# Local attention scores as 32 queries x 64 keys in two column halves, two small vector steps on GpSimd, and a load ahead of two stores

## The chip, the cores and the metric

The kernel runs on one core of a Trainium2 chip. TensorE (PE) multiplies matrices, VectorE (DVE), ScalarE (ACT) and GpSimd (POOL) work on vectors, SyncE (SP) issues most DMAs. The metric is the device time of one execution in microseconds (us), the median of several.

## What is computed

The inputs are q, k, v of shape (4, 8, 576, 64) (batch, heads, sequence, head width), eight experts' weights and the weights of a last layer.

```python
scores = scale * np.matmul(q, k.transpose(0, 1, 3, 2))          # scale = 1 / 8
rel = pos[:, None] - pos[None, :]
mask_local = (rel >= 0) & (rel < 32)                             # heads 0 to 3
mask_strided = (rel >= 0) & (pos[None, :] % 32 == pos[:, None] % 32)   # heads 4 to 7
scores = np.where(mask, scores, -1e9)
scores = scores - np.max(scores, axis=-1, keepdims=True)
attn = np.exp(scores)
attn = attn / (np.sum(attn, axis=-1, keepdims=True) + 1e-09)
x = np.matmul(attn, v)                                           # 2304 tokens x 512
# each token goes to one of 8 experts: argmax of cosine similarities / tau, weighted by its probability
out[mask] = gate_w[mask, None] * (np.maximum(x[mask] @ w1[e], 0) @ w2[e])
h = np.maximum(np.maximum(x @ w1, x @ w2), x @ w3)               # last layer
return h @ w_out
```

A local query sees only the 32 keys up to its own position.

## The kernel before

The program has three stages: attention with the routing of its tokens (to about 122 us), the experts (to about 346 us) and the last layer. Each engine works through its own list in the order in which the program is written; an instruction that waits holds up all that stand behind it on its engine. Engines wait for each other by semaphores.

**Attention** works through 44 groups, 11 for each of the 4 batches: 5 local ones (four blocks of 64 queries of a pair of heads, the fifth with two blocks) and 6 strided ones (heads are handled separately, in groups of 4, 4 and 2 blocks). `attention` is one loop over steps s, and each step writes a stage of a different group on each engine: scores of group s (`g_scores`: PE), maximum and exponentials of group s-1 (`g_max`, `g_exp`), normalisation of s-2 (`g_norm`), transposes of s-4 (`g_trans`), weighted sum of values of s-5 (`g_av`). Between them come `tok_half` (a matmul that turns the result back into token rows, whose copy to SBUF is written a step later) and the routing of the batch before (`route_stages`).

One step, engine by engine:

- PE: the scores s (L383, for a local group after a matmul that writes the mask, L375), the transposes t (L422), the token rows r (L476), the weighted sum x (L441).
- DVE: maximum mx (L390), its scaled negative nb (L394), sum of the exponentials plus 1e-9, r2 (L411, shown as `r`), reciprocal ri (L413), copy of token rows (L486), copy pt of the transposes (L424), then routing, if there is any.
- ACT: the copy xt of the weighted sum (L451), four exponentials with their row sums rs (L402), squares for the routing (L512).
- POOL: the exponentials times ri (L414), and once a batch the square root of the norms (L528) and an addition (L529).

A local group takes a block's 64 queries of two heads as 128 rows (the query tile `ql` holds zeros in the other head's half of the contraction) and 96 keys, 32 before the block and 64 in it. The keys and queries of a batch have one buffer each, so the loads of the next batch (`load_kq`, on SP's queue) wait for the last scores that read the old ones.

**The experts** and **the last layer** are chains of matmuls in which PE hardly stops. Weights are loaded, split into two parts on ACT and DVE (`w_stages`), and the nine slices of the last layer's first matmul (`UP`) are also stored to `u_scr`, from which they come back for later blocks.

Of the kernel before, what the change touches and what calls it, by code (L numbers as in the profile page):

```python
# [9 lines left out]
F32 = mybir.dt.float32  # L10
# [5 lines left out]
ALU = mybir.AluOpType  # L16
# [3 lines left out]
B, H, S, D = 4, 8, 576, 64  # L20
NT, DM, E, F, F2 = 2304, 512, 8, 1024, 768
NTILE = NT // 128
SCALE = 0.125
# [26 lines left out]
LA = 5  # L50
# [19 lines left out]
def kernel(ctx, tc, a, out, x_scr, w_scr, u_scr, perm_scr, gate_scr, upto="all"):  # L70
    nc = tc.nc
# [34 lines left out]
    UP = range(8 * E, 8 * E + 9)  # L106
# [41 lines left out]
    def w_stages():  # L148

        n = next_split[0]  # L150
        next_split[0] += 1
        t = staged.pop(n)[0]
        u, parts, ws = unit(n), [t], []
        if n in UP:

            (a11, a21), (a12, a22) = ([t.rearrange("p (k c g n) -> p k g c n", k=2, c=2, g=2)[:, k, g] for g in range(2)] for k in range(2))
            sb = pools["sb"].tile([128, 3, 256], F32, tag="sb", name="sb")  # L160
            s1, s2, s4 = (sb[:, i].rearrange("p (c n) -> p c n", c=2) for i in range(3))
            parts.append(sb.rearrange("p i n -> p (i n)"))

        def sums():
            if n in UP:
                for o, x, y, op in ((s1, a21, a22, ALU.add), (a21, a11, a21, ALU.subtract), (s2, s1, a11, ALU.subtract), (s4, a12, s2, ALU.subtract)):
                    nc.vector.tensor_tensor(out=o, in0=x, in1=y, op=op)

        def upper():
            for i, x in enumerate(parts):  # L170
                m = 1024 - 256 * i
                ws.append(slot_tile(u + i))
                nc.scalar.activation(out=ws[i][:, 0, 0:m], in_=x, func=ACTF.Copy)  # L173

        def rest():
            for i, x in enumerate(parts):
                m = 1024 - 256 * i
                nc.vector.tensor_tensor(out=ws[i][:, 1, 0:m], in0=x, in1=ws[i][:, 0, 0:m].bitcast(F32), op=ALU.subtract)  # L178
                if n in UP:
                    nc.sync.dma_start(out=u_scr[n - 8 * E, i, :, :, 0:m], in_=ws[i][:, :, 0:m].bitcast(F32))  # L180
            wsl[n] = ws if n in UP else ws[0]
            ready.add(n)
            w_load()

        return [sums, upper, rest]

# [156 lines left out]
    groups = []  # L343
# [25 lines left out]
    def g_scores(g):  # L369
        b, kind, j, hh = groups[g]  # L370
        ns, nq, nk = shape(g)
        ps = ps_s.tile([128, 512], F32, tag="s", name="s")
        if kind == 0:
            o = 96 if j == 0 else 0 if j == 2 else 192
            nc.tensor.matmul(  # L375
                out=ps[:, 0:ns * nk], lhsT=identb, rhs=mask_l[:, o:o + ns * nk], start=True, stop=False, skip_group_check=True)
        for i in range(ns):
            c, blk = slot(g, i)
            if kind == 0:
                q, k = ql[:, c, 128 * blk:128 * blk + 128], kl[:, c, 64 * blk:64 * blk + 96]  # L380
            else:
                q, k = (t[:, hh, c, 126 * blk:126 * blk + nq] for t in (qs, ks))
            nc.tensor.matmul(  # L383
                out=ps[:nq, i * nk:(i + 1) * nk], lhsT=q, rhs=k, start=kind == 1, stop=kind == 1 or i == ns - 1, skip_group_check=True)
        st[g] = dict(ps=ps)

    def g_max(g):
        ns, nq, nk = shape(g)
        mx = st_p.tile([128, 4], F32, tag="mx", name="mx")
        nc.vector.tensor_reduce(  # L390
            out=mx[:nq, 0:ns], in_=st[g]["ps"][:nq, 0:ns * nk].rearrange("p (s k) -> p s k", s=ns),
            axis=AX.X, op=ALU.max, negate=True)
        nb = st_p.tile([128, 4], F32, tag="nb", name="nb")
        nc.vector.tensor_scalar(out=nb[:nq, 0:ns], in0=mx[:nq, 0:ns], scalar1=SCALE, scalar2=None, op0=ALU.mult)  # L394
        st[g]["nb"] = nb

    def g_exp(g):
# [9 lines left out]
    def g_norm(g):  # L407
        ns, nq, nk = shape(g)
        d = st[g]
        r2 = st_p.tile([128, 4], F32, tag="r2", name="r2")  # L410
        nc.vector.tensor_scalar(out=r2[:nq, 0:ns], in0=d["rs"][:nq, 0:ns], scalar1=1e-9, scalar2=None, op0=ALU.add)  # L411
        ri = st_p.tile([128, 4, 1], F32, tag="ri", name="ri")
        nc.vector.reciprocal(out=ri[:nq, 0:ns, 0], in_=r2[:nq, 0:ns])  # L413
        nc.gpsimd.tensor_tensor(  # L414
            out=d["p"][:nq, 0:ns, :nk], in0=d["p"][:nq, 0:ns, :nk],
            in1=ri[:nq, 0:ns].to_broadcast([nq, ns, nk]), op=ALU.mult)
# [11 lines left out]
    def g_av(g):  # L428
        b, kind, j, hh = groups[g]
        if kind == 1 and hh == 0:  # L430
            return
        ns, nq, nk = shape(g)
        if j == 0:
            xT[b, kind] = xt_p.tile([128, 2, S], F32, tag=f"xt{kind}", name="xt")
        xp = ps_x.tile([128, 512], F32, tag="x", name="x")
        n = nq if kind else 64
        for i in range(ns):
            c, blk = slot(g, i)
            for h2 in range(2):
                pt = st[g - 1 + h2]["pt"][:nk, i, :nq] if kind else st[g]["pt"][:nk, i, 64 * h2:64 * h2 + 64]  # L440
                nc.tensor.matmul(  # L441
                    out=xp[64 * h2:64 * h2 + 64, i * n:(i + 1) * n],
                    lhsT=vv[b, kind][:nk, 2 * c + h2, blk, :], rhs=pt, start=True, stop=True)
        if kind == 0:
            dst = xT[b, 0].rearrange("p c n -> p (c n)")[:, 256 * j:256 * j + 64 * ns]
            src = xp[:, 0:64 * ns]
        else:
            r0, nr = (14 * j, 14) if j < 2 else (28, 4)
            dst = xT[b, 1].rearrange("p c (a r) -> p c r a", r=32)[:, :, r0:r0 + nr, :]
            src = xp[:, 0:ns * nq].rearrange("p (c r a) -> p c r a", c=2, a=18)  # L450
        later.append(lambda: nc.scalar.activation(out=dst, in_=src, func=ACTF.Copy))  # L451
        del st[g]
        if kind:
            del st[g - 1]
# [248 lines left out]
    def attention():  # L703
# [3 lines left out]
        for s in range(NG + LA + 1):  # L707
            flush(later)
            on_act[0] = s >= NG + OA
            if s < NG:  # L710
                g_scores(s)
            if 0 <= s - 1 < NG:
                g_max(s - 1)
                g_exp(s - 1)
            if 0 <= s - LN < NG:
                g_norm(s - LN)
            flush(later_v)
            if 0 <= s - LT < NG:
                g_trans(s - LT)
            for _ in range(RATE.get(s - NG, 1)):  # L720
                if toks:
                    toks.pop(0)()
            if s >= NG:
                flush(later_v)
            if 0 <= s - LA < NG:
                g_av(s - LA)
                b, k = divmod(s - LA, 11)
                if k in (4, 10):
                    ts = range(first_tile[b], first_tile[b] + n_tiles[b])
                    toks += [lambda: None] * (DT if s < NG - 6 else 0) + [lambda i=i, k=k: tok_half(i, k // 6) for i in ts]  # L730
                if k == 10:
                    toks.append(lambda b=b: todo.extend(route_stages(b)))
                if s >= NG:
                    flush(later)
            if 0 <= s - E1 < 4:
                (embed0, embed1, embed2, embed3)[s - E1]()
            if s < NG and loads and s % 11 in (0, 5):
                if s:
                    load_kq(*loads[0], ((0, 2, 0, S),))
            if s < NG and loads and s % 11 in (4, 10):  # L740
                load_v(*loads.pop(0))
            if s in (S0, S0 + 1):
                c_load()
            if S0 < s < NG:
                now[0] += 2500
                c_after()
                if c_n[0] < CA:
                    c_before()
            for _ in range(TP):
                if todo and s >= last[0] + todo[0][0]:  # L750
                    todo.pop(0)[1]()
                    last[0] = s
# [548 lines left out]
def host_inputs(inputs):  # L1301
# [10 lines left out]
    qt[:, 2:] = qt[:, 2:][..., perm]  # L1312
    qt = qt.reshape(B, 2, 2, 128, S).transpose(0, 1, 3, 2, 4)
    ar["qs"] = qt[:, 1]
    ql = np.zeros((B, 2, 64, 2, 9, 2, 64), np.float32)
    for hh in range(2):
        ql[:, hh, :, :, :, hh] = qt[:, 0].reshape(B, 2, 64, 2, 9, 64)[:, hh]
    ar["ql"] = ql.reshape(B, 128, 2, 2 * S)
    kt = t(k)
    ar["ktl"] = np.pad(kt[:, :2], ((0, 0), (0, 0), (0, 0), (32, 0))).transpose(0, 2, 1, 3)  # L1320
# [28 lines left out]
    cb = np.ones((128, 256), np.float32)  # L1349
    cb[:, 0:128] = np.triu(np.ones((128, 128)), 1)  # L1350
    rel = np.arange(64)[:, None] - np.arange(96)[None, :] + 32
    ml = np.tile(np.where((rel >= 0) & (rel < 32), 0.0, -1e9), (2, 1))
    ml0 = np.where(np.arange(96)[None, :] < 32, -1e9, ml)
    mk = np.zeros((128, 804), np.float32)
    mk[:, 0:128] = np.eye(128)
# [32 lines left out]
```

## Time and profile before

| | us |
|---|---|
| median of 3 runs | 639.75 (635.66 to 641.02) |
| the profiled execution | 637.21 |
| its span | 635.5 |
| PE busy in it | 608.7 (96%) |
| DVE busy | 449.2 (71%) |
| ACT busy | 337.5 (53%) |
| POOL busy | 137.0 (22%) |

The profile is one execution. Busy times are shares of the whole span, and they say little of a stage: what bounds a stage is read from the chain of work that ended last and from the waits in that stage. Starts are in us from the start of the span. An instruction can start a little before the one ahead of it has ended on its engine, so a row's duration is longer than what it adds to the engine's line; the distance from start to start is what it costs there.

### The profile page before, as it was taken

To read this page: it belongs to the slowest core of one execution; us is meant where nothing else is said; L and a number is where in the kernel's file an instruction comes from. 1 tells how busy PE (TensorE), PEld (TensorE's weight loads), DVE (VectorE), ACT (ScalarE), POOL (GpSimd) and SP (SyncE) were. 2 spreads that over 40 slices of the span, in tenths; PEclk is the share of its full clock that TensorE was granted. 3 is DMA by queue.
4 is the path that set the end of the run, shared out by engine and by line. 5 is a ranking of instruction groups with operands and counts; after the bars stand their busy time and mean duration, and the time that the engine had idled before them with its cause. 6 is when DMAs were issued, how large, how long until landed. Compare 5 with 4: busy or idle time off the path is not lost.

```text
span 635.5 us, 11938 instructions
## 1 busy us (share of the span) xinstructions
PE 608.7 (96%) x4281; PEld 573.3 (90%) x4282; DVE 449.2 (71%) x1011; ACT 337.5 (53%) x909; POOL 137.0 (22%) x133
## 2 busy tenths in 40 slices
PE   6899998799999999999999999999999999999995
PEld 5788887599999999999998999988999988999984
DVE  7768988676899788979899978777344375335440
ACT  4678777555676647566666634546322256221252
POOL 5434434245414133222310000002000012000011
PEclk9999999799999999999999999999999999999998
DMA  9998672584979696778774958911376301477111
GB/s 237 290 228 230 216 189 69 181 283 147 344 277 341 180 349 221 258 250 261 269 253 154 370 243 285 371 50 59 111 265 235 117 34 58 136 264 262 44 50 54
DMA packets 44880, 130.81 MB, mean 206 GB/s; under 512 B 4632, under 2 KB 15512, under 8 KB 41456
## 3 DMA queue, kind: packets, MB, share of 16 engines
q1 hardware_dynamic: 41792, 120.50, 56.9%
q0 software_dynamic: 3024, 9.49, 4.0%
q8 instruction: 36, 0.59, 0.4%
q14 instruction: 28, 0.23, 0.1%
HBM read 97.73 MB, written 32.24 MB: 205 GB/s over the span
## 4 chain that ended last, share of the span: by engine, by line
PE 77%; DVE 10%; DMA 7%; issue 2%; ACT 2%; SPq 1%; POOL 0%; POOLq 0%; DVEq 0%
PE g L830 57%; PE q L830 10%; DMA qs<-qs 4%; PE s L383 2%; PE x L441 2%; PE r L476 2%; DVE w L178 1%; PE q L813 1%; PE t L422 1%; DMA out<-r,perm_i 1%; DMA stage<-w 1%; DVE pt L424 1%; DVE h L850 1%; DVE mx L390 1%; DMA em<-emb 1%
## 5 line engine op out<-in xcount | busy, mean ns | idle before, releaser
L830 PE MATMUL g<-xc,w 128*128 128x384 f32 x1134 | 198.1, 335 | 0.0
L830 PEld LDWEIGHTS g<-xc,w 128*128 128x128 f32 x1134 | 196.5, 188 | 1.2 <-ACT yt L1128 0.5
L178 DVE TENSOR_TENSOR w<-stage,w 128x1024 fp32r<-128x1024 f32 x76 | 105.5, 1404 | 16.7 <-ACT w L173 16.0
L830 PE MATMUL g<-h,w 128*128 128x376 f32 (+7 forms) x768 | 111.7, 301 | 1.5 <-DVE h L850 1.5
L830 PEld LDWEIGHTS g<-h,w 128*128 128x128 f32 x768 | 104.7, 189 | 2.5 <-DVE h L850 1.8
L830 PE MATMUL g<-xw,w 128*128 128x376 f32 (+7 forms) x768 | 106.0, 298 | 0.5 <-ACT xw L805 0.3
L830 PEld LDWEIGHTS g<-xw,w 128*128 128x128 f32 x768 | 104.3, 189 | 0.9 <-ACT xw L805 0.6
L173 ACT ACTIVATE w<-stage 128x1024 fp32r<-128x1024 f32 x76 | 78.7, 1055 | 9.6 <-DMA stage<-w 8.1
L1179 POOL DMA_INDIRECT out<-r,perm_i x18 | 17.5, 974 | 279.6 <-ACT r L1178 197.1
L830 PE MATMUL q<-w,hs 128*128 128x512 f32 x324 | 74.9, 390 | 1.3 <-DVE hs L1167 1.3
L830 PEld LDWEIGHTS q<-w,hs 128*128 128x128 f32 x324 | 60.5, 188 | 14.8 <-DVE hs L1167 2.6
L402 ACT ACTIVATE p<-s,nb 128x96 f32<-128x96 f32 (+2 forms) x152 | 50.8, 348 | 20.1 <-DVE r L411 15.1
L246 POOL TENSOR_TENSOR f<-f,c 128x512 int32<-128x512 int32 x24 | 34.1, 1420 | 110.1 <-DVE f L244 77.1
L1128 ACT ACTIVATE yt<-g 128x384 f32<-128x384 f32 x27 | 13.3, 492 | 72.0 <-PE g L830 46.7
L1115 DVE TENSOR_TENSOR tmp<-g,yt 128x384 f32<-128x384 f32 x36 | 19.9, 555 | 43.2 <-PE g L830 43.2
L414 POOL TENSOR_TENSOR p<-p,ri 128x384 f32<-128x384 f32 (+3 forms) x44 | 36.0, 818 | 60.1 <-DVE ri L413 44.9
L849 ACT ACTIVATE h<-g 128x376 fp32r<-128x376 f32 (+7 forms) x64 | 25.5, 409 | 28.1 <-PE g L830 26.1
L424 DVE COPY pt<-t 96x512 f32<-96x512 f32 (+3 forms) x44 | 25.5, 581 | 10.5 <-PE t L422 10.4
L968 DVE TENSOR_TENSOR xc<-yt,xc 128x384 fp32r<-128x384 f32 x42 | 21.4, 554 | 15.9 <-ACT xc L967 15.9
L864 ACT ACTIVATE yt<-g 128x376 f32<-128x376 f32 (+7 forms) x32 | 13.2, 414 | 35.6 <-PE g L830 33.7
L402 ACT ACTIVATION_READ_ACCUMULATOR p<-s,nb 128x1 f32 (+2 forms) x152 | 31.2, 205 | 0.0
L850 DVE SCALAR_TENSOR_TENSOR h<-g,h 128x376 fp32r<-128x376 f32 (+7 forms) x64 | 27.1, 451 | 5.1 <-ACT h L849 5.1
(175 smaller groups left out, 786.9 us busy)
## 6 DMA issues: line engine op xcount, KB each, us to landing
stage<-w SPq DMA_DIRECT2D x64, 512.0 KB
c<-wm SPq DMA_DIRECT2D x24, 512.0 KB
w<-u_scr SPq DMA_DIRECT2D x12, 1024.0 KB
u_scr<-w SPq DMA_DIRECT2D x9, 1024.0 KB
w<-u_scr SPq DMA_DIRECT2D x12, 768.0 KB
u_scr<-w SPq DMA_DIRECT2D x9, 768.0 KB
w_scr<-f SPq DMA_DIRECT2D x24, 256.0 KB
stage<-w_scr SPq DMA_DIRECT2D x12, 512.0 KB
```

The source lines that it names most:

```text
L173: nc.scalar.activation(out=ws[i][:, 0, 0:m], in_=x, func=ACTF.Copy)
L178: nc.vector.tensor_tensor(out=ws[i][:, 1, 0:m], in0=x, in1=ws[i][:, 0, 0:m].bitcast(F32), op=ALU.subtract)
L246: nc.gpsimd.tensor_tensor(out=f, in0=f, in1=low, op=ALU.add)
L402: nc.scalar.activation(out=p[:nq, i, :nk], in_=st[g]["ps"][:nq, i * nk:(i + 1) * nk], func=ACTF.Exp, bias=st[g]["nb"][:nq, i:i + 1], scale ...
L414: nc.gpsimd.tensor_tensor(out=d["p"][:nq, 0:ns, :nk], in0=d["p"][:nq, 0:ns, :nk], in1=ri[:nq, 0:ns].to_broadcast([nq, ns, nk]), op=ALU.mult)
L424: nc.vector.tensor_copy(out=pts[:nk, 0:ns, :nq], in_=pt[:nk, 0:ns * nq].rearrange("p (s q) -> p s q", s=ns))
L830: nc.tensor.matmul(out=ps, lhsT=ws(i), rhs=xs(j), start=first and n == 0, stop=last and n == 2, skip_group_check=more)
L849: nc.scalar.activation(out=h[:, 0], in_=ps, func=ACTF.Relu)
L850: nc.vector.scalar_tensor_tensor(out=h[:, 1], in0=ps, scalar=0.0, in1=h[:, 0].bitcast(F32), op0=ALU.max, op1=ALU.subtract)
L968: nc.vector.tensor_tensor(out=x[:, 1], in0=src[c], in1=x[:, 0].bitcast(F32), op=ALU.subtract)
L1115: nc.vector.tensor_tensor(out=tmps[i], in0=ps, in1=s, op=ALU.add)
L1179: nc.gpsimd.indirect_dma_start(out=out, out_offset=bass.IndirectOffsetOnAxis(ap=perm_i[:, col:col + 1], axis=0), in_=r, in_offset=None)
```

## The change

1. **Local scores.** A local block's 128 rows are reordered into two halves of 64 (32 queries of each of two heads), and each half is multiplied with its own 64 keys, into its own 64 partitions of the result: 8 matmuls of 64 x 64 in a group in place of 4 of 128 x 96. The rows of `ql` and the mask are laid out anew on the host, and `g_av` reads its columns by a new pattern. The mask matmul stays where it was, and the scores themselves go into a new function, `g_halves`, called behind `g_av` at the end of the step. Strided scores stay at the start of the step.
2. **Small steps on GpSimd.** nb (now L409) and r2 (now L426) are issued on POOL and no longer on DVE.
3. **A load ahead of stores.** For the nine `UP` slices the next load from `w_scr` is issued behind the first of two subtractions, and both stores to `u_scr` behind the second.

```diff
 def rest():
     for i, x in enumerate(parts):
         m = 1024 - 256 * i
         nc.vector.tensor_tensor(out=ws[i][:, 1, 0:m], in0=x, in1=ws[i][:, 0, 0:m].bitcast(F32), op=ALU.subtract)
-        if n in UP:
-            nc.sync.dma_start(out=u_scr[n - 8 * E, i, :, :, 0:m], in_=ws[i][:, :, 0:m].bitcast(F32))
+        if i == 0:
+            w_load()
+    if n in UP:
+        for i, w in enumerate(ws):
+            m = 1024 - 256 * i
+            nc.sync.dma_start(out=u_scr[n - 8 * E, i, :, :, 0:m], in_=w[:, :, 0:m].bitcast(F32))
     wsl[n] = ws if n in UP else ws[0]
     ready.add(n)
-    w_load()
...
 def g_scores(g):
...
+    st[g] = dict(ps=ps)
     if kind == 0:
         o = 96 if j == 0 else 0 if j == 2 else 192
         nc.tensor.matmul(out=ps[:, 0:ns * nk], lhsT=identb, rhs=mask_l[:, o:o + ns * nk], start=True, stop=False, skip_group_check=True)
+        return
...
+def g_halves(g):
+    b, kind, j, hh = groups[g]
+    if kind:
+        return
+    ps, ns = st[g]["ps"], shape(g)[0]
+    for i in range(ns):
+        c, blk = slot(g, i)
+        for u in range(2):
+            o = 128 * blk + 64 * u
+            nc.tensor.matmul(
+                out=ps[64 * u:64 * u + 64, 96 * i + 32 * u:96 * i + 32 * u + 64], lhsT=ql[:, c, o:o + 64],
+                rhs=kl[:, c, o // 2:o // 2 + 64], start=False, stop=i == ns - 1, skip_group_check=True)
 def g_max(g):
...
-    nc.vector.tensor_scalar(out=nb[:nq, 0:ns], in0=mx[:nq, 0:ns], scalar1=SCALE, scalar2=None, op0=ALU.mult)
+    nc.gpsimd.tensor_scalar(out=nb[:nq, 0:ns], in0=mx[:nq, 0:ns], scalar1=SCALE, scalar2=None, op0=ALU.mult)
 def g_norm(g):
...
-    nc.vector.tensor_scalar(out=r2[:nq, 0:ns], in0=d["rs"][:nq, 0:ns], scalar1=1e-9, scalar2=None, op0=ALU.add)
+    nc.gpsimd.tensor_scalar(out=r2[:nq, 0:ns], in0=d["rs"][:nq, 0:ns], scalar1=1e-9, scalar2=None, op0=ALU.add)
     ri = st_p.tile([128, 4, 1], F32, tag="ri", name="ri")
     nc.vector.reciprocal(out=ri[:nq, 0:ns, 0], in_=r2[:nq, 0:ns])
...
     if 0 <= s - LA < NG:
         g_av(s - LA)
+    if s < NG:
+        g_halves(s)
+    if 0 <= s - LA < NG:
         b, k = divmod(s - LA, 11)
```

The order of instructions around the change, from the program of each kernel. POOL, before, in the third batch (each `p` is one group's multiplication by ri):

```order
L414 TENSOR_TENSOR p<-p,ri 128x4x96 x4
L414 TENSOR_TENSOR p<-p,ri 128x2x96
L414 TENSOR_TENSOR p<-p,ri 126x4x126 x4
L414 TENSOR_TENSOR p<-p,ri 72x2x72 x2
L414 TENSOR_TENSOR p<-p,ri 128x4x96
L528 TENSOR_TENSOR nrm<-ssq,ca 128x5
```

POOL of the change, three steps around its fifth local group (`r_` and a number is r2):

```order
L409 TENSOR_SCALAR nb<-mx 128x2
L426 TENSOR_SCALAR r_1190<-rs 128x4
L429 TENSOR_TENSOR p<-p,ri 128x4x96
L409 TENSOR_SCALAR nb<-mx 126x4
L426 TENSOR_SCALAR r_1236<-rs 128x2
L429 TENSOR_TENSOR p<-p,ri 128x2x96
L409 TENSOR_SCALAR nb<-mx 126x4
L426 TENSOR_SCALAR r_1284<-rs 126x4
L429 TENSOR_TENSOR p<-p,ri 126x4x126
```

In each step nb of the newer group now stands ahead of r2 of the older one, and the multiplication behind both. DVE, before, one step of strided groups in the same batch:

```order
L390 TENSOR_REDUCE mx<-s 126x4
L394 TENSOR_SCALAR nb<-mx 126x4
L411 TENSOR_SCALAR r_1230<-rs 126x4
L413 RECIPROCAL ri<-r_1230 126x4
L486 COPY row<-r 128x272
L424 COPY pt<-t 96x512
```

DVE of the change, the same step:

```order
L405 TENSOR_REDUCE mx<-s 126x4
L428 RECIPROCAL ri<-r_1284 126x4
L504 COPY row<-r 128x272
L439 COPY pt<-t 96x512
L405 TENSOR_REDUCE mx<-s 126x4
```

The reciprocal follows the maximum directly, and its operand now comes from POOL. PE, before, two steps of local groups:

```order
L375 MATMUL s<-masks 128x384
L383 MATMUL s<-kl,ql 128x96 x4
L422 MATMUL t<-cf,p 126x126 x4
L476 MATMUL r<-rhs_i,xt 128x136 x2
L441 MATMUL x<-pt,v 64x126 x8
L375 MATMUL s<-masks 128x384
```

PE of the change, the same place:

```order
L379 MATMUL s<-masks 128x384
L437 MATMUL t<-cf,p 126x126 x4
L494 MATMUL r<-rhs_i,xt 128x136 x2
L459 MATMUL x<-pt,v 64x126 x8
L398 MATMUL s<-kl,ql 64x64 x8
L379 MATMUL s<-masks 128x384
```

The scores of a local group stand at the end of its step, behind the weighted sum, and the mask alone at its start.

## Rows read from the trace of the kernel before

**Rows 1.** Busy time of each engine by stretch (start:end, length, then each engine).
```profile
core 0: us, PE busy (x) PEld busy (x) DVE busy (x) ACT busy (x) POOL busy (x), PEclk, DMA share, GB/s
43.50:53.80 10.30, 10.26 (x127) 9.11 (x128) 8.25 (x29) 8.12 (x39) 3.77 (x5) 1.00 0.82 262
96.00:106.50 10.50, 9.36 (x117) 8.00 (x115) 9.97 (x35) 8.09 (x39) 4.12 (x4) 1.00 0.34 101
```

**Rows 2.** Chain that ended last, in order of time (start, us, what).
```profile
26.36 17.05 DMA qs<-qs
...
50.52 0.62 PE x L441 x16
...
54.08 0.86 PE s L383 x8
...
106.61 0.17 DVE nb L394
```

**Rows 3.** Timeline of DVE, one strided step (start, us, engine, line, operation).
```profile
71.55 0.68 DVE L390 TENSOR_REDUCE mx<-s 126x4 f32<-126x504 f32 x1
72.26 0.17 DVE L394 TENSOR_SCALAR nb<-mx 126x4 f32<-126x4 f32 x1
72.34 0.17 DVE L411 TENSOR_SCALAR r<-rs 126x4 f32<-126x4 f32 x1
72.54 0.18 DVE L413 RECIPROCAL ri<-r 126x4 f32<-126x4 f32 x1
72.63 0.41 DVE L486 COPY row<-r 128x272 f32<-128x272 f32 x1
72.96 0.68 DVE L424 COPY pt<-t 96x512 f32<-96x512 f32 x1
73.56 0.67 DVE L390 TENSOR_REDUCE mx<-s 126x4 f32<-126x504 f32 x1
```

**Rows 4.** Waits from 44 to 84 us (who, for whom: total us, times, longest).
```profile
DVE pt L424 <- PE t L422: 3.0, 5, 0.8
```

**Rows 5.** Timeline of POOL, as rows 3; in brackets the idle time before.
```profile
0.28 0.10 POOL L1372 MEMSET const-float32-0.0<- 128x1 f32 x1
0.31 0.10 POOL L1372 MEMSET const-float32-1.0<- 128x1 f32 x1
...
21.93 0.59 POOL L689 TENSOR_TENSOR es<-es,ca 8x1 f32<-8x1 f32 x1
22.63 0.27 POOL L690 TENSOR_SCALAR es<-es,tau_c 8x1 f32<-8x1 f32 x1
...
72.89 1.03 POOL L414 TENSOR_TENSOR p<-p,ri 126x504 f32<-126x504 f32 x1 [2.38 <-PE r L476]
```

**Rows 6.** Timeline of POOL around the second batch's norms.
```profile
86.95 1.20 POOL L528 TENSOR_TENSOR nrm<-ssq,ca 128x5 f32<-128x5 f32 x1
88.24 0.24 POOL L529 TENSOR_SCALAR nr<-nrm 128x5 f32<-128x5 f32 x1
88.57 0.83 POOL L414 TENSOR_TENSOR p<-p,ri 128x384 f32<-128x384 f32 x1
89.94 0.83 POOL L414 TENSOR_TENSOR p<-p,ri 128x384 f32<-128x384 f32 x1 [0.55 <-DVE ri L413]
```

**Rows 7.** Timeline of PE: transposes that waited for POOL's last multiplication.
```profile
90.84 0.61 PE L422 MATMUL t<-cf,p 128*96 128x128 f32 x4 [0.38 <-POOL p L414]
```

**Rows 8.** Timeline of DVE in the same stretch: one maximum, and one nb.
```profile
86.45 0.54 DVE L390 TENSOR_REDUCE mx<-s 128x4 f32<-128x384 f32 x1
...
88.68 0.74 DVE L394 TENSOR_SCALAR nb<-mx 128x4 f32<-128x4 f32 x1
```

**Rows 9.** Line 394 from 44 to 110 us: count, ns (min/median/max), first and last start.
```profile
L394 DVE TENSOR_SCALAR nb<-mx x27: 164/170/736, 46.4 to 106.6; 126x4 f32<-126x4 f32 x11, 128x4 f32<-128x4 f32 x8, 72x2 f32<-72x2 f32 x6, 128x2 f32<-128x2 f32 x2
```

**Rows 10.** Timeline of PE: the scores that waited at the end of the loads.
```profile
43.54 1.11 PE L383 MATMUL s<-ks,qs 128*126 128x126 f32 x8 [0.21 <-DMA qs<-qs]
```

**Rows 11.** Busy time as rows 1, while the last layer's slices are prepared.
```profile
346.00:420.00 74.00, 73.84 (x450) 73.29 (x451) 60.10 (x101) 36.49 (x65) 0.00 (x0) 1.00 0.77 288
```

More of the change, by code (lines that the diff above doesn't have):

```diff
@@ L376, in g_scores @@
                 out=ps[:, 0:ns * nk], lhsT=identb, rhs=mask_l[:, o:o + ns * nk], start=True, stop=False, skip_group_check=True)
+            return
         for i in range(ns):
             c, blk = slot(g, i)
[L379 to L385, printed above, removed]
+            q, k = (t[:, hh, c, 126 * blk:126 * blk + nq] for t in (qs, ks))
+            nc.tensor.matmul(out=ps[:nq, i * nk:(i + 1) * nk], lhsT=q, rhs=k, start=True, stop=True, skip_group_check=True)
+    def g_halves(g):
[10 more added lines that the diff above has]
+                    rhs=kl[:, c, o // 2:o // 2 + 64], start=False, stop=i == ns - 1, skip_group_check=True)
     def g_max(g):
@@ L439, in g_av @@
             for h2 in range(2):
-                pt = st[g - 1 + h2]["pt"][:nk, i, :nq] if kind else st[g]["pt"][:nk, i, 64 * h2:64 * h2 + 64]
+                if kind:
+                    pt = st[g - 1 + h2]["pt"][:nk, i, :nq]
+                else:
+                    pt = st[g]["pt"][:nk, i].rearrange("k (u h q) -> k h u q", u=2, h=2)[:, h2]
                 nc.tensor.matmul(
@@ L1314, in host_inputs @@
     ar["qs"] = qt[:, 1]
-    ql = np.zeros((B, 2, 64, 2, 9, 2, 64), np.float32)
+    ql = np.zeros((B, 2, 64, 2, 18, 2, 32), np.float32)
     for hh in range(2):
-        ql[:, hh, :, :, :, hh] = qt[:, 0].reshape(B, 2, 64, 2, 9, 64)[:, hh]
+        ql[:, hh, :, :, :, hh] = qt[:, 0].reshape(B, 2, 64, 2, 18, 32)[:, hh]
     ar["ql"] = ql.reshape(B, 128, 2, 2 * S)
@@ L1351, in host_inputs @@
     rel = np.arange(64)[:, None] - np.arange(96)[None, :] + 32
-    ml = np.tile(np.where((rel >= 0) & (rel < 32), 0.0, -1e9), (2, 1))
+    ml = np.where((rel >= 0) & (rel < 32), 0.0, -1e9).reshape(2, 1, 32, 96).repeat(2, 1).reshape(128, 96)
     ml0 = np.where(np.arange(96)[None, :] < 32, -1e9, ml)
```

## The prediction, word for word

> **What bounds the kernel now.** I read the page first: PE is busy 96% of the span, so from the experts on only PE's own work counts. The change leaves those matmuls alone; three of its parts sit in attention and one in the preparation of the last layer's slices. So I read these stretches one by one: busy time by stretch, the chain of waits through each, then the lines of DVE and POOL step by step.
>
> In the first 43 us the chain runs through loads. It shows one load of queries, issued at 26.36, that takes 17.05 us to land [rows 2], and the scores that need it start at 43.54 after a wait of 0.21 us for it [rows 10]. From there to about 54 us PE is full (10.26 of 10.30 us), and DVE is close behind (8.25) [rows 1]. In the third batch's local groups the chain still passes through PE's scores, but it ends with DVE's own line, up to the last nb at 106.61 [rows 2], where DVE is busy 9.97 of 10.50 us and PE 9.36 [rows 1]. So PE and DVE are nearly equal limits here, and DVE has little to give: from 44 to 84 us it waited for transposes 3.0 us in all, 5 times [rows 4].
>
> One strided step on DVE takes 2.01 us, from the maximum at 71.55 to the next at 73.56 [rows 3]. The maximum ends at 72.23, and the reciprocal starts at 72.54: the two small instructions between them cost DVE 0.31 us.
>
> **The small steps on GpSimd.** DVE gives up nb and r2, but its next instruction is the reciprocal, which reads r2. On POOL r2 stands behind the newer group's nb, which needs the maximum that DVE has just finished. So in every step DVE now waits from the end of the maximum until POOL has been woken, has done both, and has woken DVE. Nothing on DVE can pass the waiting reciprocal; behind it stand the row copy, the copy of the transposes, the next maximum.
>
> The price, from rows: from the end of ri (72.54 + 0.18 = 72.72, rows of DVE) to POOL's start at 72.89 is 0.17 us [rows 3, 5]. POOL's addition on 128x5 takes 0.24 us [rows 6]; I take that for nb and again for r2. Back from POOL, the multiplication that ends at 89.94 + 0.83 = 90.77 releases transposes at 90.84: 0.07 us [rows 6, 7]. Sum 0.17 + 0.24 + 0.24 + 0.07 = 0.72 us, in place of 0.31: each step is **0.41 us longer**.
>
> The floor: two of POOL's memsets start 0.03 us apart [rows 5]; if r2 can overlap nb like that, the gap is 0.17 + 0.03 + 0.24 + 0.07 = 0.51 and the step 0.20 longer. The ceiling: the 8x1 operation takes 0.27, starts 0.11 after the end of the one before it (21.93 + 0.59 = 22.52 to 22.63) [rows 5], and the way back costs as much as the way there: 0.17 + 0.27 + 0.11 + 0.27 + 0.17 = 0.99, or 0.68 longer. I take 0.41, because the addition on 128x5 is the same operation on nearly the same tile.
>
> The Trainium skill (Perfetto Trace Analysis, GPSIMD Engine Instruction) says that a GpSimd span is unreliable, and that consecutive instructions are to be timed from start to start. By that rule the floor is the better price, since only the memsets stand so in this trace. No pair of small arithmetic instructions is there to decide it.
>
> Steps that count: 27 nb start between 46.4 and 106.6 [rows 9], each with one reciprocal behind it. 27 x 0.41 = 11.1 us. DVE's 3.0 us of waits for transposes [rows 4] take up as much of it: **+8.1**.
>
> Two corrections on POOL's queue. The norms take POOL from 86.95 to 88.48 (88.24 + 0.24) [rows 6], while a maximum ends at 86.45 + 0.54 = 86.99 [rows 8]. Its nb could start 0.17 later, at 87.16, and now waits until 88.48: 1.3 us, with ACT's exponentials and DVE behind it. The first batch's norms come after a shorter multiplication and before a longer step; for them I choose 0.3. Together **+1.6**. On the other side, DVE's nb at 88.68 took 0.74 us against a median of 0.17 [rows 8, 9]; it ended at 89.42, when POOL's multiplication of 88.57 had just ended at 89.40 [rows 6]. That stall goes with nb: **-0.6**.
>
> **The local scores.** A local group's scores take 0.86 us on the chain; the weighted sum, already 16 instructions with 64 output columns each, takes 0.62 [rows 2]. The new scores have that form with 128 contraction rows for 96, so I take 0.62: 0.24 less a group. Behind 43.5 us stand two batches of 4.5 such groups, 2.2 us of PE's time. If they ran on in PE's own line that would be the gain; but once DVE's step is 2.4 us long PE waits for DVE, so I count 0 of it, and keep 2.2 for the rivals. Standing last in the step, the scores must be done before the next maximum: after DVE's copy of the transposes PE has the weighted sum (0.62, more for a strided group) and the scores (0.62), while DVE has a maximum (0.54), the gap (0.72), a row copy (0.33 from start to start) and a copy (0.60) [rows 3, 8]: 1.2 or somewhat more against 2.2, so it is covered. Without that cover DVE would stall once more in each local step.
>
> **Before 43.5 us** each step also gets longer, about ten of them behind the wait for the load. The cover is the load itself, which spends 17 us in the queues whatever PE does. I count 0; if that cover is too short, it costs up to 10 x 0.41 = 4.1 us. PE does gain something there: the mask no longer has scores behind it that wait for keys, so transposes can pass. That ends at the same load.
>
> **The load ahead of the stores.** SP's queue gets the next slice one subtraction sooner and the stores later. PE is busy 73.84 of 74.00 us while it happens [rows 11], so nothing is to be won; the stores are read back a whole block later. 0. Should a load come later than it does now, PE's 0.16 us of slack would be the cover.
>
> **Sum**, on the profiled execution: 637.2 + 8.1 + 1.6 - 0.6 = 646.3. That execution lies 2.5 us under the median of 639.75 and inside the runs' 635.66 to 641.02; the mean of all four is 638.4, which gives 647.5. I say **647**.
>
> **The rivals.**
> - *The floor price.* POOL overlaps the two small steps: 27 x 0.20 = 5.4, minus 3.0, plus 1.6, minus 0.6 = +3.4: 641 on the profiled execution, 642 on the mean. For it: the memsets. Against it: the two steps wait on different engines (DVE for nb, ACT for r2), and POOL's other rows stand nearly end to end. 22%.
> - *Faster.* If POOL needed at most 0.31 - 0.17 - 0.07 = 0.07 us for both steps, DVE's line would be no longer than now. That is the point from which it decides. Then the stall of 0.6 goes, and PE's 2.2 us show where PE is the limit: 637.2 - 2.8 = 634.4. For it: the memsets' spacing of 0.03. Against it: every arithmetic row on POOL, 0.24 us and more. 8%.
> - *The ceiling price*, with the front uncovered: 27 x 0.68 = 18.4, minus 3.0, plus 1.6, minus 0.6 = +16.4, and part of the 4.1: 654 to 657. For it: the 0.11 us between POOL's 8x1 rows. Against it: that pair is dependent, nb and r2 aren't. 14%.
> - My forecast, a step 0.3 to 0.55 us longer, has 56%: 27 times that, less 2.0, is +6 to +13.
>
> A measurement of this kernel tells about 1% (6.4 us) from no change. The forecast falls almost all beyond it, its lower edge inside; the floor stays within 1%; half of the faster case is below 633.4. So slower 0.58, same 0.36, faster 0.06. The range goes from the floor case to the upper part of the forecast: 640 to 653.
>
> **What will show it.** Right: in attention DVE's reciprocals wait for POOL's r2, some 0.4 us at a time; from the maximum's end to ri 0.7 us; the start of the experts 8 to 10 us later, and equal durations behind it. A local group's scores take 0.6 us, and their maximum does not wait. Wrong: ri starts within 0.3 us of the maximum; or the longest waits are the maxima's for late scores; or the load at 43 us lands later by as much as the steps before it grew; or PE idles in the last layer.

## The result, and the profile after

The changed kernel takes 646.92 us in the median of 6 runs (646.65 to 650.62); the kernel before had 640.23 beside it (6 runs, 635.66 to 642.38). The ratio is 1.0129, with a 95% interval of 1.0093 to 1.0166: slower by about 1%. The profiled execution took 646.83 us with a span of 645.1, against 637.2 and 635.5 before.

To find the place I use one milestone of the program in all kernels: the start of VectorE's second maximum in the second strided batch, **A**, and the start of the last group's maximum, **B**. A is at 45.73 us before and 47.84 after, B at 106.28 and 115.98. So in these two executions the front is 2.1 us later, the 26 steps from A to B take 68.14 us for 60.55 (**+7.6**), and from B to the end it is 529.1 us for 529.2. All of it lies in attention.

VectorE's timeline of the changed kernel, the strided step that answers to [rows 3]:

```profile
75.96 0.68 DVE L405 TENSOR_REDUCE mx<-s 126x4 f32<-126x504 f32 x1
77.29 0.18 DVE L428 RECIPROCAL ri<-r 126x4 f32<-126x4 f32 x1 [0.65 <-POOL r L426]
77.39 0.41 DVE L504 COPY row<-r 128x272 f32<-128x272 f32 x1
77.71 0.68 DVE L439 COPY pt<-t 96x512 f32<-96x512 f32 x1
78.31 0.67 DVE L405 TENSOR_REDUCE mx<-s 126x4 f32<-126x504 f32 x1
```

GpSimd's timeline of the same step, and of the second batch's norms, which answers to [rows 6]:

```profile
76.73 0.23 POOL L409 TENSOR_SCALAR nb<-mx 126x4 f32<-126x4 f32 x1 [1.83 <-DVE mx L405]
77.03 0.23 POOL L426 TENSOR_SCALAR r<-rs 126x4 f32<-126x4 f32 x1
77.62 1.03 POOL L429 TENSOR_TENSOR p<-p,ri 126x504 f32<-126x504 f32 x1 [0.36 <-DVE ri L428]
...
92.56 1.20 POOL L546 TENSOR_TENSOR nrm<-ssq,ca 128x5 f32<-128x5 f32 x1
93.84 0.25 POOL L547 TENSOR_SCALAR nr<-nrm 128x5 f32<-128x5 f32 x1
94.18 0.23 POOL L409 TENSOR_SCALAR nb<-mx 128x4 f32<-128x4 f32 x1
94.48 0.23 POOL L426 TENSOR_SCALAR r<-rs 128x4 f32<-128x4 f32 x1
```

The step takes 2.35 us where it took 2.01. Between the maximum's end (76.64) and the reciprocal VectorE now does nothing for 0.65 us: 0.09 until GpSimd starts nb, 0.30 from nb's start to r's, 0.23 for r, 0.03 back. Before, it spent 0.31 us there on the two instructions themselves. GpSimd had been idle for 1.83 us when nb came, and ScalarE's last sum for r had been there since 75.26 us (75.05 + 0.21), so r could have been done long before; it stands behind nb.

The waits of the changed kernel from 44 to 84 us (who, for whom: total us, times, longest) say the same for all steps; in [rows 4] the longest wait of VectorE was the one for transposes:

```profile
DVE ri L428 <- POOL r L426: 11.0, 16, 1.2
POOL nb L409 <- DVE mx L405: 10.2, 11, 1.8
ACT p L417 <- POOL nb L409: 9.1, 11, 1.6
```

The busy time of the second stretch of [rows 1], in the changed kernel:

```profile
core 0: us, PE busy (x) PEld busy (x) DVE busy (x) ACT busy (x) POOL busy (x), PEclk, DMA share, GB/s
96.00:106.50 10.50, 10.50 (x100) 9.46 (x98) 7.02 (x25) 5.40 (x27) 3.98 (x11) 0.74 0.26 75
```

VectorE, relieved of two instructions in each step, is busy 7.02 us where it was 9.97, and yet the work comes later: at the same time from its start the changed kernel is some 9 us behind in its program. TensorE's 10.50 of 10.50 is no full load: its granted clock there is 0.74, and before it was 1.00.

The chain of waits of the changed kernel (start, us, what; answers to [rows 2]) shows what now sets the length of this step:

```profile
76.05 0.59 DVE mx L405
76.65 0.08 issue
76.73 0.23 POOL nb L409
76.95 0.08 issue
77.03 0.23 POOL r L426
77.27 0.02 issue
77.29 0.18 DVE ri L428
77.47 0.33 DVE row L504
77.79 0.59 DVE pt L439
...
87.52 0.64 PE s L398 x16
```

One turn of the step runs through VectorE and GpSimd, and no piece of it is TensorE's. Before, the chain from 68 to 80 us was TensorE's alone, busy 16.90 us of the 16.90 from 68.0 to 84.9; now it is busy 14.90 of them. The last row is a local group's scores in halves, 0.64 us where 0.86 stood.

### The profile page after: what moved, and what is told of

The parts are those of the page before. It is cut to its first block, busy times and chain, and to the rows that moved or that the text cites. A ratio compares the mean times of both kernels' runs of the same rounds, so it can differ in the third digit from the quotient of the medians.

```text
span 645.1 us, 12176 instructions
## 1 busy us (share of the span) xinstructions
PE 611.6 (95%) x4425; PEld 572.3 (89%) x4426; DVE 435.4 (67%) x923; ACT 337.8 (52%) x909; POOL 158.4 (25%) x221
## 4 chain that ended last, share of the span: by engine, by line
PE 73%; DVE 10%; DMA 8%; issue 3%; POOL 3%; ACT 2%; SPq 1%; POOLq 0%; DVEq 0%
PE g L851 57%; PE q L851 9%; DMA qs<-qs 3%; DMA out<-r,perm_i 2%; DMA v<-vl 2%; PE s L385 1%; DVE w L178 1%; PE x L459 1%; PE q L834 1%; PE r L494 1%; DVE pt L439 1%; DMA em<-emb 1%; POOL p L429 1%; DMA stage<-w 1%; PE t L437 1%
## 5 line engine op out<-in xcount | busy, mean ns | idle before, releaser
L249 POOL TENSOR_TENSOR f<-f,c 128x512 int32<-128x512 int32 x24 | 34.9, 1452 | 108.5 <-DVE f L247 80.3
L815 POOL DMA_INDIRECT xg<-x_scr,win_i x22 | 26.1, 1186 | 23.8 <-PE q L965 6.9
```

What stands on the lines that cost most here:

```text
L249: nc.gpsimd.tensor_tensor(out=f, in0=f, in1=low, op=ALU.add)
L815: nc.gpsimd.indirect_dma_start(out=t[i][:r], out_offset=None, in_=x_scr, in_offset=bass.IndirectOffsetOnAxis(ap=win_i[:r, NWIN * e + i:NWI ...
```

## The experiments

Each kernel was timed against the kernel before on the same chip, and the ratio is to that; from the profile stand A and the way from A to B. "Small steps" are nb and r.

| kernel | small steps on GpSimd | ratio, 95% interval | A, us | A to B, us |
|---|---|---|---|---|
| before | none | 1 | 45.73 | 60.55 |
| before, second profile | none | (one run) | 43.06 | 60.54 |
| changed | nb, then r | 1.0129 [1.0093, 1.0166] | 47.84 | 68.14 |
| changed, second profile | nb, then r | (one run) | 46.10 | 67.86 |
| small steps only | nb, then r | 1.0096 [1.0062, 1.0131] | 44.50 | 67.16 |
| scores and load only | none | 0.9990 [0.9960, 1.0019] | 44.28 | 59.74 |
| load only | none | 0.9996 [0.9970, 1.0022] | 44.11 | 60.53 |
| r ahead of nb | r, then nb | 0.9990 [0.9957, 1.0023] | 46.35 | 61.28 |
| nb on GpSimd | nb | 0.9984 [0.9958, 1.0009] | 47.12 | 59.65 |
| r on GpSimd | r | 0.9961 [0.9923, 0.9999] | 46.83 | 59.20 |
| one more step | nb, a copy of r, r | 1.0288 [1.0235, 1.0341] | 48.80 | 74.53 |
| without r | none | 0.9953 [0.9920, 0.9987] | 45.49 | 57.73 |
| nb on GpSimd, without r | nb | 0.9927 [0.9896, 0.9958] | 45.44 | 60.98 |

**The small steps alone.** The kernel before, with the two lines of the change:

```diff
-        nc.vector.tensor_scalar(out=nb[:nq, 0:ns], in0=mx[:nq, 0:ns], ...)
+        nc.gpsimd.tensor_scalar(out=nb[:nq, 0:ns], in0=mx[:nq, 0:ns], ...)
...
-        nc.vector.tensor_scalar(out=r2[:nq, 0:ns], in0=d["rs"][:nq, 0:ns], ...)
+        nc.gpsimd.tensor_scalar(out=r2[:nq, 0:ns], in0=d["rs"][:nq, 0:ns], ...)
```

> The kernel before with one part of the change: the maxima's scaling (nb) and the sums' addition (r) on GpSimd. Theory (each of VectorE's steps now waits for r, which stands on GpSimd's queue behind nb, which needs the maximum VectorE has just finished; the trace of the changed kernel shows 0.65 us from the maximum's end to the reciprocal where 0.31 stood): 27 steps x 0.34 = 9.2 us, plus 2.0 for two normalizations ahead on the queue, less up to 3.0 us of waits for transposes that it absorbs: 645 to 649 us, with reciprocals waiting about 0.65 us for r in the profile. Rival (the time went into the late local scores or the moved load, and the new waits are only where VectorE would have waited anyhow): 639 to 642 us.

645.00 us against 638.83. These two lines bring 6.6 of the 7.6 us from A to B, with the same 0.65 us ahead of the reciprocal. Step by step from A to B this kernel and the changed one have equal lengths within 0.03 us in 22 of 26 steps: once GpSimd's chain sets the step, the shorter scores buy nothing.

**The other two parts alone.** The changed kernel with those two lines back on VectorE:

> The changed kernel with nb and r back on VectorE, so the scores in halves and the moved load alone. Theory: the wait goes and the chain of steps stands as in the kernel before, TensorE has some 0.2 us less in each local step, which hides: 636 to 641 us, gap from maximum to reciprocal 0.31 us again. Rival (late halves or the load cost): 643 us or more. Of the 2.1 us by which the changed kernel was late before its first strided step (45.64 where 43.54 stood): if the halves or the load cause it, this profile shows it too; if the small steps do, it does not.

637.12 us against 638.83, and 0.8 us less from A to B; the interval takes in no change. With A at 44.28, neither the halves nor the load push the front back in this profile.

**The load alone.** The kernel before with `w_load()` called after the first subtraction, ahead of the stores:

> The kernel before with one part of the change: a slice's load issued ahead of its stores. Theory: those issues wait for nothing that bounds: 639 to 641 us, the same. Rival (the stores, and the copies of the slices behind them, come later and the experts' end waits for them, or the early loads shift): 642 us or more. Also a second look at the first 43.5 us of the kernel before: the first strided scores at 43.5 if the 2.1 us in the changed kernel come from its steps, anywhere from 43 to 46 if transfers vary from run to run.

637.71 us against 638.83, a ratio of 0.9996; A to B 60.53. No effect of the load shows.

**r ahead of nb.** In the changed kernel, r is issued before the newer group's maximum and nb:

```diff
             if s < NG:
                 g_scores(s)
+            if 0 <= s - LN < NG:
+                g_r2(s - LN)
             if 0 <= s - 1 < NG:
                 g_max(s - 1)
```

> The changed kernel with r written ahead of nb, so that on GpSimd's queue it stands before nb and needs only sums of a step before. Same engines, same operations, same number. Theory (the cost is the order on GpSimd's queue): the reciprocal follows the maximum at under 0.1 us, a strided step on VectorE falls to about 1.7 us from 2.0, and the time to 632 to 640 us. Rival (the price is GpSimd's for small steps, or its hold on VectorE's port, or the late halves): 644 us or more, as the changed kernel.

638.95 us against 638.83: with the same operations on the same engines, the order alone takes the loss away. That rules out as the cost GpSimd's price, any holding up of VectorE's instructions by GpSimd's, and the late halves. But the reciprocal did not follow the maximum at under 0.1 us, as had been expected, and nothing was won. The chain of this kernel (columns as above):

```profile
74.15 0.23 POOL r L426
74.38 0.08 issue
74.46 0.23 POOL nb L409
74.69 0.02 issue
74.72 1.51 ACT p L417 x8
76.22 0.08 issue
76.30 0.23 POOL r L426
```

It is a ring of 2.15 us: r waits for the sums of ScalarE's exponentials, nb stands behind r, and the next exponentials wait for nb. The wait has moved from the maximum to the exponentials; VectorE still lost 5.2 us to r from 44 to 84 us.

**One of the two alone.** The changed kernel with r back on VectorE, and with nb back on it:

> The changed kernel with r back on VectorE: only the maxima's scaling nb on GpSimd. Theory (VectorE waited because r needs nb's turn on the queue, and nb needs the maximum): no reciprocal waits for GpSimd, nb's 0.17 us leave VectorE, the exponentials start some 0.2 us later in a step: 634 to 641 us, and reciprocals 0.2 us or less behind the maximum. Rival (any small step on GpSimd costs by its price or its hold on the port): 642 us or more.

> The changed kernel with nb back on VectorE: only the sums' addition r on GpSimd, where it is issued as soon as ScalarE's sums are there and no maximum stands ahead of it. Theory: no reciprocal waits for GpSimd, 27 steps lose 0.07 to 0.14 us each: 633 to 639 us. Rival (the hop from GpSimd to VectorE and the price there are the cost): 642 us or more, as the changed kernel. In the run with r ahead of nb the exponentials came to wait for nb, nb for r, r for the exponentials of the group before, in steps of 2.14 us; here that ring is open.

638.09 and 637.48 us against 639.15. Either small step alone on GpSimd is free within the intervals, and so are both with r in front; only the two together with nb in front cost. VectorE's timeline with r on GpSimd:

```profile
71.71 0.68 DVE L405 TENSOR_REDUCE mx<-s 126x4 f32<-126x504 f32 x1
72.42 0.17 DVE L409 TENSOR_SCALAR nb<-mx 126x4 f32<-126x4 f32 x1
72.50 0.17 DVE L428 RECIPROCAL ri<-r 126x4 f32<-126x4 f32 x1
```

Here r had run at 71.29, before the maximum started, and the reciprocal stands 0.08 us behind nb: 0.11 us from the maximum's end (72.39). It does not always go so well: from 44 to 110 us the reciprocals still waited 3.6 us for r, 9 times, where none had been expected.

**A dose.** The changed kernel with a second r, into a tile that nobody reads, between nb and r:

```diff
+        rx = st_p.tile([128, 4], F32, tag="rx", name="rx")
+        nc.gpsimd.tensor_scalar(out=rx[:nq, 0:ns], in0=d["rs"][:nq, 0:ns], ...)
         nc.gpsimd.tensor_scalar(out=r2[:nq, 0:ns], in0=d["rs"][:nq, 0:ns], ...)
```

> The changed kernel with one more small step on GpSimd between nb and r (a second r into a tile that nobody reads): a dose. Theory (maximum, nb, r, reciprocal are one chain): 0.30 us more in each of 27 steps, 0.95 us from the maximum's end to the reciprocal in place of 0.65, and 652 to 657 us. Rival (the chain has slack behind it, or the time went elsewhere): 646 to 650 us.

658.47 us against 639.15, some 1.6% more than the changed kernel's ratio, a little above the 652 to 657 expected. GpSimd's timeline, the same strided step:

```profile
80.59 0.23 POOL L409 TENSOR_SCALAR nb<-mx 126x4 f32<-126x4 f32 x1 [1.82 <-DVE mx L405]
80.90 0.24 POOL L427 TENSOR_SCALAR rx<-rs 126x4 f32<-126x4 f32 x1
81.19 0.23 POOL L428 TENSOR_SCALAR r<-rs 126x4 f32<-126x4 f32 x1
```

VectorE's reciprocal waited 0.96 us where it waited 0.65: 0.31 for one more small step. From A to B the step costs 6.4 us, 0.25 for each of 26, against the changed kernel, whose own way holds 0.8 us of a halved clock (below); against the small steps alone it is 7.4, or 0.28 each. Another 1.0 us lies in front of A and 1.1 behind B. The profiled execution, 655.30 us, is the fastest of the six; what the others lose beyond it I did not follow.

**Without r.** The reciprocal reads ScalarE's sums; nb on VectorE, then nb on GpSimd:

```diff
-        r2 = st_p.tile([128, 4], F32, tag="r2", name="r2")
-        nc.gpsimd.tensor_scalar(out=r2[:nq, 0:ns], in0=d["rs"][:nq, 0:ns], scalar1=1e-9, ...)
...
-        nc.vector.reciprocal(out=ri[:nq, 0:ns, 0], in_=r2[:nq, 0:ns])
+        nc.vector.reciprocal(out=ri[:nq, 0:ns, 0], in_=d["rs"][:nq, 0:ns])
```

> The changed kernel with nb on VectorE and without r: the reciprocal reads ScalarE's sums. What is left out is the addition of 1e-9 to sums that are 1 or more (the largest term of a row is exp(0)). Theory (a step of the attention is as long as VectorE's chain in it): 27 steps lose 0.07 to 0.14 us each against the run with both on VectorE, which had 637.1 us: 633 to 636 us, faster than the kernel before by 0.4 to 0.9%. Rival (VectorE's chain does not bound, TensorE does): 637 us.

> The changed kernel without r: nb stays on GpSimd, the reciprocal reads ScalarE's sums. What is left out is the addition of 1e-9 to sums that are 1 or more. Theory (nb on GpSimd was never the cost, r behind it was): the whole loss goes by taking r away: 633 to 639 us. Rival (nb's trip over GpSimd costs by starting the exponentials later): 1 to 3 us above the run without r that keeps nb on VectorE (637.5 us), 638 to 641.

637.46 us against 639.15, and 635.56 against 640.66. Both beat the kernel before, by 0.1 to 0.8% and by 0.4 to 1.0%; their intervals overlap, so which is better stays open. The first has the median of its rival (637) and not the 633 to 636 of its theory, while its ratio lies in the theory's 0.4 to 0.9%: alone it does not decide whether VectorE's chain or TensorE bounds there, though its A to B is 2.0 us shorter than that of the kernel with both on VectorE. The second is the changed kernel less one instruction: nb on GpSimd costs nothing that shows, and everything lost goes with r. The chain of the second:

```profile
68.88 0.61 PE x L457 x16
69.50 1.07 PE s L385 x8
70.57 0.44 PE t L435 x4
71.01 0.47 PE r L492 x4
```

It is TensorE's line again, and VectorE's longest waits from 44 to 110 us are the 9.6 us for transposes: VectorE's own line no longer bounds this stretch. Its A to B of 60.98 us holds a stretch from 84.9 to 96 us at a clock of 0.69, where the kernel with nb on VectorE had 1.00.

**Both kernels once more.**

> The kernel before once more, for a second look at its first stretch. If transfers alone move the first stretch from execution to execution, the second strided batch's second maximum starts somewhere from 44 to 48 us (45.73 in the first look), while its way from there to the last maximum stays at 60.5 us within 0.5.

> The changed kernel once more. Theory: from the second strided batch's second maximum to the last maximum 68 us again (68.14 in the first look, 60.55 in the kernel before), within 0.7. If the 2.1 us in front are the execution's and not the change's, that maximum starts anywhere from 44 to 48 us; if they are the change's, at 47.5 to 48.2 again.

A to B came out at 60.54 and 67.86 us, within 0.3 us of the first profiles, while A moved by 2.7 and 1.7 us within one kernel, to 43.06 (below the 44 to 48 expected) and 46.10. The way from B to the end moves as well: 533.8 and 531.2 us, where both had 529. So only A to B can be compared between single executions to better than some microseconds.

## Why the prediction was right, and where not

The forecast (647 us, slower) and its mechanism held; the terms of its sum did not all hold their size.

- **The wait for r, right, but too dear.** Forecast were 0.72 us from maximum to reciprocal; it is 0.65. The way there costs 0.09 us instead of 0.17, the way back 0.03 instead of 0.07, and the two steps 0.30 + 0.23 instead of 0.24 + 0.24, since 0.08 us lie between them. [rows 6] had shown such a gap: the addition at 88.24 and the multiplication behind it start 0.33 us apart, at a span of 0.24. So the step of [rows 3] is 0.34 us longer, not 0.41. Nor did every step of the kernel before get along with 0.31 us: in 15 of the 26 from A to B it was 0.37 or more, as in this step on its VectorE, where the maximum ends at 48.99:

```profile
47.72 0.69 DVE L424 COPY pt<-t 96x512 f32<-96x512 f32 x1 [0.43 <-PE t L422]
48.32 0.67 DVE L390 TENSOR_REDUCE mx<-s 126x4 f32<-126x504 f32 x1
...
49.37 0.18 DVE L413 RECIPROCAL ri<-r 126x4 f32<-126x4 f32 x1
```

  Summed over the 26 steps, the time from a maximum's end to the reciprocal is 9.95 us before and 18.98 with the small steps alone: 9.0 more, norms and stall included, where the forecast had 11.1 + 1.6 - 0.6 = 12.1. Without those two it is 7.6 for the 11.1, or 0.29 a step. This term was the one mis-sized most.
- **What the steps absorb, 3.0, was 2.4:** the 9.0 less the 6.6 by which A to B grew with the small steps alone. It is the waits for transposes, as forecast. Of the five of [rows 4] the first, 0.69 us at 45.12, lies in front of A; the others, 0.43 (above), 0.21, 0.82 and 0.80, make 2.26.
- **The norms, 1.6, were 2.0.** The reciprocal behind the first batch's norms waited 1.16 us and the one behind the second's 2.12, instead of 0.65: 0.5 and 1.5. The norms' rows above show it: nb at 94.18 comes only after nr. VectorE's row behind it:

```profile
94.75 0.18 DVE L428 RECIPROCAL ri<-r 128x4 f32<-128x4 f32 x1 [2.12 <-POOL r L426]
```

  The 0.3 chosen for the first batch was too low.
- **nb's stall, 0.6, right.** The step that held it before became 0.28 us shorter, where some 0.3 longer was due.
- **The local scores, right, counted 0 and worth 0 here.** 0.64 us for 0.62 forecast, and no maximum behind A waited for them. The cover is the longer step: with the small steps back on VectorE two maxima behind A waited 0.22 and 0.36 us for them, and even so scores and load together are worth up to 0.8 us from A to B. In front of A the forecast's cover did not hold everywhere: in the changed kernel the maxima at 12.84 and 34.65 us waited 0.81 and 1.16 us for them.
- **The load, right:** 0, by its own run; in the stretch that answers to [rows 11], 9.6 us later, TensorE is busy 73.55 of 74.00 us.
- **The granted clock was not in the sum.** From 94.6 to 101.5 us it stood at 0.50, and the two steps from 98.85 us on took 2.95 and 3.23 us where the kernel with the small steps alone, at 1.00, took 2.33 and 3.04: 0.8 us.
- **The front, counted 0, is open.** A is at 43.1 to 45.7 us in five profiles without small steps on GpSimd (mean 44.5), and at 44.5 to 47.8 in four with both there (mean 46.2). The bands overlap, and the front's loads differ between executions of one kernel: the queries of [rows 2] were issued at 26.36 and 25.39 us in the two profiles of the kernel before, at 28.60 and 28.44 in the changed one, at 26.97 in the one with the small steps alone, and at 27.37 to 27.57 in three kernels without small steps on GpSimd. In the changed kernel's first profile the load of 28.60 took 16.90 us and bounds A as forecast, only from a later start. But the cover does not always hold: in its second profile, and in the kernel with one more step, the chain from 24 us to A has no load in it, and the latter, whose chain runs through nb and r there, has the latest A of all, 48.80. By the means some 1.7 us may belong to the change; these runs don't settle it. So 0 may have been too low, inside the bound of 4.1.

From A to B the forecast said 8.1 + 1.6 - 0.6 = 9.1 and 7.6 came: 9.0 of waits, less 2.4 absorbed, plus 0.8 of clock, and 0.2 besides. The 2.1 us of the front in that execution made up the difference to the 9.6 us between the two profiles. So the mechanism was right, but that the total came so near is in part luck: a price for the wait that was 3.5 us too high stood against a clock and a front that were not counted.

Of the rivals, the floor price (0.20 a step) falls: r never overlapped nb, it starts 0.30 us behind nb's start in step after step. The two memsets 0.03 us apart [rows 5] were no measure for arithmetic on tiles, and the pair of [rows 6], 0.33 apart, would have been one. The ceiling (0.68) falls too, and the faster case, which wanted both steps within 0.07 us. That rival had a point all the same: with r out of the queue, nb on GpSimd costs nothing that shows.

The Trainium skill (Perfetto Trace Analysis, GPSIMD Engine Instruction) asks for times from start to start instead of spans. The trace agrees: nb's span is 0.23 us, and r starts 0.30 behind it. What failed was the pair of rows to which I applied it. The same section of the Trainium skill says that an instruction which reads no tensor has no start time reported; a memset reads none, so its place in this trace should not have served as a price, though no run here tells what the 0.03 us are.

## What to carry to other kernels

An instruction moved to an idle engine joins that engine's queue: ask what stands ahead of it there, what that waits for, and whether the engine that gave it away waits for the answer at once. Two small steps that were free one by one cost some 0.3 us a step together, because one needed the newest value and the other, behind it, was needed next; and swapping them closed another ring. Before moving a step, ask whether it is needed: the two kernels without r have the lowest ratios of all, though their intervals overlap those of the kernels that only place it better.

## What the runs showed of the hardware that I had not expected

GpSimd's small step costs the same on 2 columns as on 4, and on 72 partitions as on 128. nb and r, lines 409 and 426 of the changed kernel (count, ns min/median/max, first and last start, forms):

```profile
L409 POOL TENSOR_SCALAR nb<-mx x44: 217/226/237, 9.8 to 116.4; 128x4 f32<-128x4 f32 x16, 126x4 f32<-126x4 f32 x16, 72x2 f32<-72x2 f32 x8, 128x2 f32<-128x2 f32 x4
L426 POOL TENSOR_SCALAR r<-rs x44: 222/226/234, 11.6 to 117.7; 128x4 f32<-128x4 f32 x16, 126x4 f32<-126x4 f32 x16, 72x2 f32<-72x2 f32 x8, 128x2 f32<-128x2 f32 x4
```

0.226 us against VectorE's median of 0.170 for the same nb [rows 9], without VectorE's one stall of 0.736, and a hop of 0.09 us from the maximum's end to nb and 0.03 from r's end back. The hop is not one number: the multiplication still starts 0.15 us behind the reciprocal's end (77.47 to 77.62).

TensorE's granted clock fell to half between A and B, where both profiles of the kernel before have 1.00 (there it falls to 0.50 only at 119.0 and 115.0 us, where attention runs out). The busy time of the changed kernel around it (columns as in the stretches above):

```profile
94.00:96.00 2.00, 0.39 (x2) 0.41 (x3) 1.18 (x4) 1.40 (x8) 1.38 (x4) 0.66 1.05 223
96.00:98.00 2.00, 2.00 (x21) 1.51 (x20) 1.38 (x6) 1.40 (x8) 1.28 (x3) 0.50 0.84 238
98.00:100.00 2.00, 2.00 (x11) 1.98 (x11) 1.24 (x8) 0.99 (x5) 0.46 (x2) 0.50 0.07 15
100.00:102.00 2.00, 2.00 (x23) 1.74 (x21) 1.30 (x6) 0.30 (x2) 0.83 (x1) 0.63 0.00 0
```

TensorE had waited behind the norms (0.39 us busy of 2.00), and then ran at 0.50, which is 1.2 GHz, until after 100 us: the strided scores took 2.07 us there and 1.14 elsewhere. The second profile shows the same fall 2 us earlier. But the kernel with the small steps alone has 2 us with no matmul at all and stays at 1.00; it falls only at 108.5 us:

```profile
90.00:92.00 2.00, 0.00 (x0) 0.00 (x0) 0.75 (x4) 1.06 (x7) 1.40 (x5) 1.00 1.02 217
108.00:110.00 2.00, 2.00 (x16) 1.48 (x15) 1.35 (x5) 1.97 (x9) 1.52 (x4) 0.61 0.39 112
```

So such idle time comes ahead of the fall without settling it. Nor is the fall a mark of the loss: the kernel with r ahead of nb and the one with nb on GpSimd and without r, which lose nothing, have 0.50 from 91.0 to 94.4 and from 88.3 to 95.1 us. A step that delays VectorE may cost at TensorE's clock too, here 0.8 us; that the delay brings the fall about is not shown.
